# b1 rows loaded in W1's queue and transposed alone, 21 matmuls into the first layer

## The chip, the cores and the metric

The kernel runs on one core of a Trainium2 chip. The metric is device microseconds of one execution. Every execution also has a span, from the first to the last instruction of its profile; all times "at" below are microseconds from the span's start. The metric is about 2 us longer than the span.

## The reference, cut to what matters

The input x has 2048 rows of 640. A gate mixes two branches: a diagonal complex state-space layer (A) and a two-layer network (B).

```python
h = jnp.einsum("bsd,df->bsf", x, w1) + b1          # B: 640 -> 1728, bias b1
h = _gelu(h)
b = jnp.einsum("bsf,fd->bsd", h, w2) + b2          # back to 640
Lam_bar = jnp.exp(dt * Lam)                        # A: 640 states, dt = exp(log_dt)
# ... Bu = x B_bar^T; h_t = Lam_bar h_(t-1) + Bu_t; a = 2 Re(h C^T) + x Dskip
return g * a + (1 - g) * b                         # g = sigmoid(sum(x * gate_w))
```

Two kinds of small vectors are needed as columns, one value per partition: Lambda_re, Lambda_im and log_dt (15 rows of 128) for the tables of branch A, and b1 (13.5 rows of 128, padded to 14) as the bias of the GELU after the first layer.

## The kernel before: the parts that matter

Every operation is put to a list scheduler, which works with estimated durations (`dur`, `lat`) and priorities (`prio`) when the kernel is built, and fixes the program order of each engine. A late estimate therefore gives a late place in program order, whatever happens on the chip.

The small rows are loaded from ACT's queue; one TensorE transpose turns all 29 rows into columns, and VectorE copies them out of PSUM:

```python
for i, (nm, src) in enumerate((("lre", A_Lambda_re), ("lim", A_Lambda_im), ("ldt", A_log_dt))):
    load(nm, "act", ..., rows[i * KP:(i + 1) * KP, :], src..., [("rows", i)], prio=-100 + i, dur=0.45)
load("b1a", "act", ..., rows[3 * KP:NR - 1, :], B_b1[0:nmain]..., ["b1a"], prio=-97, dur=0.4, lat=2.5)
for h in range(2):                                  # the last half row, twice
    load(f"b1b{h}", "act", ..., rows[NR - 1:NR, h * 64:h * 64 + FL], ..., [("b1b", h)], prio=-96 + h, dur=0.4, lat=2.5)
# ... cut
def f_cols():
    return inc("pe", nc.tensor.transpose(psC[:, 0:NR], rows[:, :], ident[0:NR, 0:NR]))
op("cols", "pe", 0.2, [("rows", 0), ("rows", 1), ("rows", 2), "b1a", ("b1b", 0), ("b1b", 1), "ident"], [("bank", 7)], f_cols, prio=-855)
def f_cols1():
    return inc("dve", nc.vector.tensor_copy(out=cols[:, :], in_=psC[:, 0:NR]))
op("cols1", "dve", 0.2, [("bank", 7)], ["lcol", "b1col"], f_cols1, prio=-3000)
```

x's first 512 rows come in two halves (SP's queue), are transposed by 20 TensorE transposes and copied by VectorE to xT. Then the first layer starts, 35 matmuls of 128x512, block k of W1 after block k:

```python
def m1_first():
    for k in range(KD):                             # KD = 5
        for jf in ((5, 6, 0, 1, 2, 3, 4) if k == 0 else range(NW)):   # NW = 7
            # matmul(PS[jf], W1sb[:, k, jf*128:(jf+1)*128], xT[:, k, 0:512]), prio 1, 2, ... 35
    # ... cut: GELU of the 7 banks with b1col as bias
```

SP's queue issues, in this order: x (2), W1's blocks (5), W1's rest, B (10 DMA transposes), xT block 1 (5), W2, xT blocks 2 and 3 (5), C (10).

## Time and profile before

| | |
|---|---|
| time, median of 3 (range) | 217.86 us (217.44 to 218.26) |
| span of the profiled execution | 215.8 us |
| TensorE matmul (PE) busy | 212.0 us, 98% |
| VectorE (DVE) busy | 191.4 us, 89% |
| chain of waits | PE 96%, DMA 2% |

The page of the kernel before, the busy time of the engines (share of the span, number of instructions) and the shares of the chain that ended last:

```profile
...
PE 212.0 (98%) x1286; PEld 124.2 (58%) x1286; DVE 191.4 (89%) x268; ACT 99.3 (46%) x169; POOL 4.6 (2%) x13
...
PE 96%; DMA 2%; SPq 0%; DVE 0%; issue 0%
...
```

PE is busy for 98% of the span and makes 96% of the chain. Nothing is to be had from any other engine unless PE waits for it.

The timeline of the head (start, duration, engine, line, operation, out<-in, count; in brackets the idle time ahead of it and its releaser):

```profile
...
3.73 2.34 PE L413 MATMUL ps<-ident,xn 128*128 128x128 bf16 x20
...
5.25 1.09 DVE L420 COPY xT<-ps 128x512 bf16<-128x512 bf16 x3 [2.25 <-PE ps L413]
...
6.57 0.59 PE L611 MATMUL ps<-xT,W1sb 128*128 128x512 bf16 x2 [0.51 <-DMA W1sb<-in_B_w_dram]
...
7.09 0.18 PE L430 MATMUL ps<-ident,rows 29*128 29x29 bf16 x1
...
7.21 7.30 PE L611 MATMUL ps<-xT,W1sb 128*128 128x512 bf16 x33
7.32 0.19 DVE L435 CAST cols<-ps 128x29 f32<-128x29 bf16 x1 [0.98 <-PE ps L430]
...
11.34 0.32 DVE L479 TENSOR_TENSOR tr<-tr 128x165 f32<-128x165 f32 x1
...
14.34 6.64 PE L630 MATMUL ps<-xT,W1sb 128*128 128x512 bf16 x30
...
```

L413 are the x transposes, L611 the first layer, L430 the transpose of the 29 rows. It stands after the second matmul of the layer. The first matmul waits 0.51 us for a DMA of W1, not for xT, whose first copy ran from 5.25. The tables of branch A start with the copy of the columns at 7.32 (L435); their long coefficient block starts at 11.34.

The chain of waits over the head (start, duration, what):

```profile
...
1.76 4.67 DMA W1sb<-in_B_w_dram
6.43 0.14 issue
6.57 0.59 PE ps L611 x2
7.16 0.12 PE ps L430
7.28 7.23 PE ps L611 x33
14.51 6.47 PE ps L630 x30
...
```

The start of the first layer is the landing of W1's first block, issued at 1.76 and landed at 6.43. From there on the chain is PE alone.

### The profile page before, as it was taken

Reading aid. Unit: us, or ns where it says so; the run is one execution under the profiler, and the core shown is the slowest. Engines: PE = TensorE matmul, PEld = TensorE weight load, DVE = VectorE, ACT = ScalarE, POOL = GpSimd, SP = SyncE. Lnnn points to the kernel's source line nnn. Section 1 sums busy time; section 2 is a strip of 40 time slices with the busy share of each in tenths; the row PEclk is TensorE's granted clock in tenths of the full one; section 3 lists DMA queues with packets and bytes.
Section 4 is the critical chain, followed back from the end, with each engine's and each line's share of the span. In section 5 each row is a group of like instructions: output and inputs, shape, how many; then the busy total and the mean of one; then the engine's idle time right before and its main releaser. Section 6 shows DMA issues by size and latency. Waiting matters only on the chain.

```text
span 215.8 us, 3288 instructions
## 1 busy us (share of the span) xinstructions
PE 212.0 (98%) x1286; PEld 124.2 (58%) x1286; DVE 191.4 (89%) x268; ACT 99.3 (46%) x169; POOL 4.6 (2%) x13
## 2 busy tenths in 40 slices
PE   8999999999999999999999999999999999999995
PEld 4444444444577776444457777544447777777774
DVE  3799999999999999999996999799999999996313
ACT  2478556665533224556653322556662233233220
POOL 1010030000000100000000010000000000000000
DMA  6987579995610140000000013000000000001001
GB/s 191 350 158 138 93 204 338 235 126 122 124 31 30 34 149 2 30 0 0 3 0 0 33 37 147 30 3 0 0 0 3 1 34 28 30 30 33 30 30 30
DMA packets 28201, 15.44 MB, mean 72 GB/s; under 512 B 22044, under 2 KB 27740, under 8 KB 28188
## 3 DMA queue, kind: packets, MB, share of 16 engines
q1 hardware_dynamic: 27568, 12.95, 24.7%
q0 software_dynamic: 560, 2.30, 3.4%
q8 instruction: 10, 0.16, 0.3%
q14 instruction: 3, 0.02, 0.0%
q10 hardware_dynamic: 60, 0.01, 0.0%
HBM read 7.38 MB, written 2.62 MB: 46 GB/s over the span
## 4 chain that ended last, share of the span: by engine, by line
PE 96%; DMA 2%; SPq 0%; DVE 0%; issue 0%
PE ps L750 26%; PE ps L630 23%; PE ps L776 20%; PE ps L675 20%; PE ps L611 4%; DMA W1sb<-in_B_w_dram 2%; PE ps L751 2%; PE ps L651 1%; SPq L330 0%; DVE osb L809 0%; PE ps L430 0%
## 5 line engine op out<-in xcount | busy, mean ns | idle before, releaser
L750 PE MATMUL ps<-W2sb,Gl 128*128 128x320 bf16 x416 | 61.4, 299 | 0.0
L750 PEld LDWEIGHTS ps<-W2sb,Gl 128*128 128x128 bf16 x416 | 40.5, 98 | 16.6 <-issue 0.4
L630 PE MATMUL ps<-xT,W1sb 128*128 128x512 bf16 x225 | 49.2, 379 | 0.0
L776 PE MATMUL ps<-CT,H 128*128 128x320 bf16 (+2 forms) x330 | 46.1, 295 | 0.0
L715 DVE TENSOR_TENSOR_SCAN W<-atab,V 128x1280 bf16<-128x1280 f32 x16 | 44.3, 2811 | 0.3
L675 PE MATMUL ps<-xT,BT 128*128 128x512 bf16 x200 | 43.8, 379 | 0.0
L776 PEld LDWEIGHTS ps<-CT,H 128*128 128x128 bf16 x330 | 31.7, 98 | 12.0
L638 ACT ACTIVATE Gl<-ps,cols 128x512 bf16<-128x512 f32 x45 | 30.6, 692 | 16.1 <-PE ps L630 16.1
L630 PEld LDWEIGHTS ps<-xT,W1sb 128*128 128x128 bf16 x225 | 22.0, 98 | 26.6
L675 PEld LDWEIGHTS ps<-xT,BT 128*128 128x128 bf16 x200 | 19.5, 98 | 23.5 <-issue 0.4
L684 ACT ACTIVATE U<-ps 128x512 bf16<-128x512 f32 x40 | 23.9, 597 | 18.3 <-PE ps L675 18.3
L795 DVE SCALAR_TENSOR_TENSOR xg<-xn,gcol,dsk 128x640 bf16<-128x640 bf16 x16 | 13.9, 883 | 0.4
L758 ACT ACTIVATE E_0<-ps,g1col 128x320 bf16<-128x320 f32 x12 | 6.3, 527 | 16.5 <-PE ps L751 16.5
L590 DVE SCALAR_TENSOR_TENSOR scr<-xn,gwb 128x640 bf16<-128x640 bf16 x16 | 13.2, 822 | 0.4
L479 DVE TENSOR_TENSOR H<-H,V 128x1280 bf16<-128x1280 bf16 x16 | 12.5, 822 | 0.3
L479 DVE TENSOR_TENSOR V<-V,W 128x1280 bf16<-128x1280 bf16 x16 | 12.5, 821 | 0.3
L479 DVE TENSOR_TENSOR V<-mr,U 128x2560 bf16<-128x2560 bf16 x8 | 11.9, 1490 | 0.5 <-DVE s L479 0.2
L479 DVE TENSOR_TENSOR H<-c,W 128x2560 bf16<-128x2560 bf16 x8 | 11.9, 1489 | 0.1
L479 DVE TENSOR_TENSOR V<-s,W 128x2560 bf16<-128x2560 bf16 x8 | 11.9, 1484 | 0.0
L479 DVE TENSOR_TENSOR W<-mi,U 128x2560 bf16<-128x2560 bf16 x8 | 11.9, 1484 | 0.0
L758 ACT ACTIVATE E_2<-ps,g1col 128x320 bf16<-128x320 f32 x10 | 5.3, 527 | 13.6 <-PE ps L751 13.6
L758 ACT ACTIVATE E_1<-ps,g1col 128x320 bf16<-128x320 f32 x10 | 5.3, 528 | 12.9 <-PE ps L751 12.9
(89 smaller groups left out, 124.6 us busy)
## 6 DMA issues: line engine op xcount, KB each, us to landing
out_dram<-osb SPq DMA_DIRECT2D x15, 160.0 KB, 1.8
W2sb<-in_B_w_dram SPq DMA_DIRECT2D x1, 2080.0 KB, 12.7
xn<-in_A_x_dram POOLq DMA_DIRECT2D x3, 640.0 KB, 4.8
W1sb<-in_B_w_dram SPq DMA_DIRECT2D x5, 224.0 KB, 4.8
W1sb<-in_B_w_dram SPq DMA_DIRECT2D x1, 1040.0 KB, 7.5
xn<-in_A_x_dram SPq DMA_DIRECT2D x2, 320.0 KB, 3.0
xT<-in_A_x_dram SPq DMA_TRANSPOSE x10, 4.6
dsk<-in_A_Dskip_dram POOLq DMA_DIRECT2D x1, 160.0 KB, 6.9
```

The costliest lines, as they stand in the source:

```text
L479: return inc("dve", nc.vector.tensor_tensor(out=o, in0=a, in1=b, op=o_))
L590: t = inc("dve", nc.vector.scalar_tensor_tensor(out=scr[:, :], in0=xn[q % 2][:, c, :], scalar=1.0, in1=gwb[:, :], op0=ALU.mult, op1=ALU.mu ...
L611: return inc("pe", nc.tensor.matmul(PS[jf][:, :], W1sb[:, k, jf * 128:(jf + 1) * 128], xT[:, k, 0:512], start=(k == 0), stop=(k == KD - 1)))
L630: t = nc.tensor.matmul(PS[bank][:, :], W1sb[:, k, jf * 128:(jf + 1) * 128], xT[:, k, q * 512:(q + 1) * 512], start=(k == 0), stop=(k == KD ...
L638: return inc("act", nc.scalar.activation(Gl[q % 2][:, jf, :], PS[bank][:, :], ACT.Gelu_apprx_tanh, bias=b1col[:, jf:jf + 1]))
L675: t = nc.tensor.matmul(PS[bank][:, :], BT[:, kd, ci, k * 128:(k + 1) * 128], xT[:, kd, q * 512:(q + 1) * 512], start=(kd == 0), stop=(kd = ...
L684: return inc("act", nc.scalar.activation(dst, src, ACT.Copy, scale=1.0 if ci == 0 else -1.0))
L715: t = inc("dve", nc.vector.tensor_tensor_scan(out=g[:, ci, :], data0=a, data1=v[:, ci, :], initial=0.0, op0=ALU.mult, op1=ALU.add))
L750: t = nc.tensor.matmul(PS[bank][:, 0:HALF], Gl[q % 2][:, jf, ts], W2sb[:, jf, cols], start=(jf == 0), stop=False)
L758: return inc("act", nc.scalar.activation(E1[c % NE][:, cols], PS[bank][:, 0:HALF], ACT.Copy, scale=g1col[:, c:c + 1]))
L776: t = nc.tensor.matmul(PS[bank][:, 0:n], H[b % NHB][:, ci, k, s * 128:(s + 1) * 128], CT[:, k, ci, cols], start=(i == 0), stop=(i == 2 * K ...
L795: return inc("dve", nc.vector.scalar_tensor_tensor(out=xg[c % 2][:, :], in0=xn[q % 2][:, c % 4, :], scalar=gcol[:, c:c + 1], in1=dsk[:, :] ...
```

## The change

Intent: the transpose of Lambda and dt no longer waits for b1, so it can run before the first layer and the tables of branch A can start earlier; b1, which is not needed before the first GELU at 13, is loaded later, out of ACT's queue, and transposed by itself 21 matmuls into the layer.

```diff
-        rows = SB("rows", [NR, 128], BF16)
-        cols = SB("cols", [128, NR], FP32)
+        rows = SB("rows", [3 * KP, 128], BF16)
+        b1rows = SB("b1rows", [NF, 128], BF16)
+        cols = SB("cols", [128, 3 * KP], FP32)
+        b1col = SB("b1col", [128, NF], FP32)
 ...
-        load("b1a", "act", ..., prio=-97, dur=0.4, lat=2.5)
-        for h in range(2):
-            load(f"b1b{h}", "act", ..., prio=-96 + h, dur=0.4, lat=2.5)
+        load("b1a", "sp", "l_b1a", b1rows[0:NF - 1, :], B_b1[0:nmain]..., ["b1a"], prio=6.2, dur=0.3, lat=2.5)
+        load("b1b", "sp", "l_b1b", b1rows[NF - 1:NF, :]..., B_b1[nmain:F]....broadcast_to([1, 2, FL]), ["b1b"], prio=6.3, dur=0.3, lat=2.5)
 ...
-            return inc("pe", nc.tensor.transpose(psC[:, 0:NR], rows[:, :], ident[0:NR, 0:NR]))
-        op("cols", "pe", 0.2, [("rows", 0), ("rows", 1), ("rows", 2), "b1a", ("b1b", 0), ("b1b", 1), "ident"], ...)
+            return inc("pe", nc.tensor.transpose(psC[:, 0:3 * KP], rows[:, :], ident[0:3 * KP, 0:3 * KP]))
+        op("cols", "pe", 0.2, [("rows", 0), ("rows", 1), ("rows", 2), "ident"], ...)
 ...
+        def f_colb():
+            return inc("pe", nc.tensor.transpose(psC[:, 0:NF], b1rows[:, :], ident[0:NF, 0:NF]))
+        op("colb", "pe", 0.1, ["b1a", "b1b", "ident"], [("bank", 7)], f_colb, prio=21.5)
+        def f_colb1():
+            return inc("dve", nc.vector.tensor_copy(out=b1col[:, :], in_=psC[:, 0:NF]))
+        op("colb1", "dve", 0.2, [("bank", 7)], ["b1col"], f_colb1, prio=-1000)
```

More of the change, by code (lines that the diff above doesn't have):

```diff
@@ L240, in bass_gated_mix__ssm_conv_s5__dense_activation_gelu__prompt_kernel @@
         gwb = SB("gwb", [128, D], BF16)
-        NR = 3 * KP + NF
-        rows = SB("rows", [NR, 128], BF16)
-        cols = SB("cols", [128, NR], FP32)
-        lcol = cols[:, 0:3 * KP].rearrange("p (a k) -> p a k", a=3)
-        b1col = cols[:, 3 * KP:NR]
+        rows = SB("rows", [3 * KP, 128], BF16)
+        b1rows = SB("b1rows", [NF, 128], BF16)
+        cols = SB("cols", [128, 3 * KP], FP32)
+        lcol = cols[:, :].rearrange("p (a k) -> p a k", a=3)
+        b1col = SB("b1col", [128, NF], FP32)
         dtb = SB("dtb", [128, KP], BF16)
@@ L358, in bass_gated_mix__ssm_conv_s5__dense_activation_gelu__prompt_kernel @@
             load(nm, "act", "l_" + nm, rows[i * KP:(i + 1) * KP, :], src.rearrange("(k p) -> k p", p=128), [("rows", i)], prio=-100 + i, dur=0.45)
-        load("b1a", "act", "l_b1a", rows[3 * KP:NR - 1, :], B_b1[0:nmain].rearrange("(j p) -> j p", p=128), ["b1a"], prio=-97, dur=0.4, lat=2.5)
-        for h in range(2):
-            load(f"b1b{h}", "act", f"l_b1b{h}", rows[NR - 1:NR, h * 64:h * 64 + FL], B_b1[nmain:F].rearrange("(j p) -> j p", j=1), [("b1b", h)],
-                 prio=-96 + h, dur=0.4, lat=2.5)
+        load("b1a", "sp", "l_b1a", b1rows[0:NF - 1, :], B_b1[0:nmain].rearrange("(j p) -> j p", p=128), ["b1a"], prio=6.2, dur=0.3, lat=2.5)
+        load("b1b", "sp", "l_b1b", b1rows[NF - 1:NF, :].rearrange("j (h p) -> j h p", h=2),
+             B_b1[nmain:F].rearrange("(j h p) -> j h p", j=1, h=1).broadcast_to([1, 2, FL]), ["b1b"], prio=6.3, dur=0.3, lat=2.5)
         def f_iota():
@@ L429, in f_cols @@
         def f_cols():
-            return inc("pe", nc.tensor.transpose(psC[:, 0:NR], rows[:, :], ident[0:NR, 0:NR]))
-        op("cols", "pe", 0.2, [("rows", 0), ("rows", 1), ("rows", 2), "b1a", ("b1b", 0), ("b1b", 1), "ident"], [("bank", 7)], f_cols, prio=-855)
+            return inc("pe", nc.tensor.transpose(psC[:, 0:3 * KP], rows[:, :], ident[0:3 * KP, 0:3 * KP]))
+        op("cols", "pe", 0.2, [("rows", 0), ("rows", 1), ("rows", 2), "ident"], [("bank", 7)], f_cols, prio=-855)
         def f_cols1():
-            return inc("dve", nc.vector.tensor_copy(out=cols[:, :], in_=psC[:, 0:NR]))
-        op("cols1", "dve", 0.2, [("bank", 7)], ["lcol", "b1col"], f_cols1, prio=-3000)
+            return inc("dve", nc.vector.tensor_copy(out=cols[:, :], in_=psC[:, 0:3 * KP]))
+        op("cols1", "dve", 0.2, [("bank", 7)], ["lcol"], f_cols1, prio=-3000)
+        def f_colb():
[4 more added lines that the diff above has]
+        op("colb1", "dve", 0.2, [("bank", 7)], ["b1col"], f_colb1, prio=-1000)
         def f_dt():
```

## The prediction

> **What bounds the kernel.** TensorE. The page has PE busy 212.0 of 215.8 us (98%), and the chain of waits is PE for 96%, DMA 2%. VectorE is 89% busy, but the table of waits shows no PE wait on it after the first layer has begun. Time can be won only in the first 6.6 us, or where something is squeezed between matmuls.
>
> The head, from the timeline, the chain and the trace's records of DMA semaphores: the x halves land at 3.57 and 4.51 us; 20 transposes run 3.73 to 6.07; the first matmul starts at 6.57, released by the first W1 block, which lands at 6.44 (the chain shows 4.67 us of that DMA). xT block 0 is copied by about 5.7, so that side has 0.7 us of slack. The transpose of the 29 rows stands after the second matmul: matmuls start 0.216 us apart, the third would start at 7.00 and starts at 7.21. So it costs PE about 0.2 us (0.12 on the chain). All its rows had landed by 5.81 (b1) and 4.49 (Lambda, dt): no wait, just a late place in program order. The Trainium skill, "TensorE: Matmul & The Clock Gate", Step-by-step, says matmuls stay in program order, only weight loads are pulled ahead; this fits.
>
> **What the change does.**
> 1. Three b1 loads leave ACT's queue (0.92 us of issue, nothing waits for it).
> 2. Two small loads enter SP's queue behind W1's five blocks: about 0.3 us of issue each, so W1's rest and the B transposes are issued 0.6 us later. W1's rest landed at 11.71, first used 14.34: slack 2.6. B_re is used from 20.82, landed 16.64; B_im used about 26.4, landed 23.79; xT1 used 31.6, landed 29.20. All have 2 us or more. The b1 rows stand in ring order behind W1 (the skill, "DMA: Bandwidth & Descriptors", Queues, rings and completion order), whose fifth block landed at 8.71: I estimate 9 us, before their transpose at about 11.2.
> 3. The Lambda/dt transpose no longer waits for b1; the list scheduler should place it between the two halves of the x transposes. Rows landed at 4.49, its turn is about 4.8: no stall. It delays the second half by 0.15 to 0.3 us, inside the 0.7 us of slack.
> 4. A new 14-row transpose sits after 21 matmuls: about 0.1 to 0.2 us of PE, the same as is removed.
> 5. VectorE: the first COPY to cols moves from 7.32 to about 5.2; the Lambda chain (dtb, acol, angles) starts about 0.8 us earlier. But the new b1 copy is queued ahead of the long coefficient block and waits for the transpose (about 11.4), so VectorE idles about 0.8 us there and the block starts at about 11.6, against 11.34. The gain is given back. The tables then end within 0.4 us of 33.7, and their first user is far from PE's path (first H ready at 49, needed 61.5).
>
> **Sum.** Out of the first layer about -0.2 us, into it +0.15; start unchanged (6.57, W1). Net 0 to -0.1 us; the spread of the three runs (217.44 to 218.26) is larger. Predicted 217.8 us, range 217.2 to 218.4; faster by over 2% 1%, within 2% 98%, slower 1%.
>
> **To check.** First matmul 6.4 to 6.7; Lambda transpose before 5.2; one gap of about 0.1 to 0.2 us after matmul 21; VectorE idle just before the b1 copy with TensorE's transpose as releaser; last first-layer matmul ends at 14.5; PE share 98%.
>
> **What would make it wrong.** The small rows in ACT's queue landing late, holding the x transposes past 6.4 (PE start moves one for one); b1 landing after 11 behind the 128-partition W1 blocks, stalling PE; the b1 copy placed behind the coefficient block, holding banks for 2 us; a different order later.

## The result

The changed kernel takes 217.51 us (median of 6, 217.20 to 217.69); the kernel before takes 217.82 us (6 runs, 217.44 to 218.26). The ratio is 0.9986, 95% interval 0.9972 to 1.0000. A ratio is the mean time of one kernel's runs over that of the other's of the same rounds, so it is not quite the ratio of the medians quoted.

The page of the changed kernel, the same lines (its lines of code have moved: first layer L621, x transposes L412, Lambda transpose L429, b1 transpose L439):

```profile
...
PE 212.0 (98%) x1287; PEld 123.6 (57%) x1287; DVE 191.5 (89%) x269; ACT 99.3 (46%) x169; POOL 4.6 (2%) x13
...
PE 96%; DMA 2%; SPq 0%; DVE 0%; issue 0%
...
```

The timeline of its head:

```profile
...
3.96 1.24 PE L412 MATMUL ps<-ident,xn 128*128 128x128 bf16 x10
...
5.12 0.18 PE L429 MATMUL ps<-ident,rows 15*128 15x15 bf16 x1
...
5.23 0.73 PE L412 MATMUL ps<-ident,xn 128*128 128x128 bf16 x10
5.34 0.17 DVE L434 CAST cols<-ps 128x15 f32<-128x15 bf16 x1 [2.34 <-PE ps L429]
...
6.57 4.71 PE L621 MATMUL ps<-xT,W1sb 128*128 128x512 bf16 x21 [0.60 <-DMA W1sb<-in_B_w_dram]
...
11.21 0.18 PE L439 MATMUL ps<-ident,b1rows 14*128 14x14 bf16 x1
...
11.42 0.17 DVE L444 CAST b1col<-ps 128x14 f32<-128x14 bf16 x1 [0.86 <-PE ps L439]
11.51 0.56 DVE L489 TENSOR_TENSOR tr<-tr 128x165 f32<-128x165 f32 x2
...
14.35 6.64 PE L640 MATMUL ps<-xT,W1sb 128*128 128x512 bf16 x30
...
```

The chain of waits over its head:

```profile
...
1.76 4.67 DMA W1sb<-in_B_w_dram
6.43 0.14 issue
6.57 4.71 PE ps L621 x21
11.28 0.11 PE ps L439
11.39 3.13 PE ps L621 x14
14.51 6.47 PE ps L640 x30
...
```

The two chains agree to the hundredth: W1's first block lands at 6.43 in both, the layer starts at 6.57 in both, and the next layer starts on the chain at 14.51 in both. One small transpose has gone from matmul 2 to matmul 21 (0.12 and 0.11 us on the chain). On VectorE the first column copy moved from 7.32 to 5.34 and the table chain ran ahead, but the b1 copy (L444) stands in front of the coefficient block and waited 0.86 us for the b1 transpose; the block started at 11.51 in place of 11.34. So the profiles show the whole change, and none of the 0.3 us: the spans are 215.8 before and 215.9 after. What was left to find out was whether the 0.3 us are real, and if so where they lie.

### The profile page after: what moved, and what is told of

Its sections match the earlier page's. It is cut to its first block, busy times and chain, and to the rows that moved or that the text cites. A ratio compares the mean times of both kernels' runs of the same rounds, so it can differ in the third digit from the quotient of the medians.

```text
span 215.9 us, 3291 instructions
## 1 busy us (share of the span) xinstructions
PE 212.0 (98%) x1287; PEld 123.6 (57%) x1287; DVE 191.5 (89%) x269; ACT 99.3 (46%) x169; POOL 4.6 (2%) x13
## 4 chain that ended last, share of the span: by engine, by line
PE 96%; DMA 2%; SPq 0%; DVE 0%; issue 0%
PE ps L760 26%; PE ps L640 22%; PE ps L786 20%; PE ps L685 20%; PE ps L621 4%; DMA W1sb<-in_B_w_dram 2%; PE ps L761 2%; PE ps L661 1%; SPq L330 0%; DVE osb L819 0%; PE ps L439 0%
## 5 line engine op out<-in xcount | busy, mean ns | idle before, releaser
L786 PE MATMUL ps<-CT,H 128*128 128x320 bf16 (+2 forms) x330 | 46.1, 295 | 0.0
L786 PEld LDWEIGHTS ps<-CT,H 128*128 128x128 bf16 x330 | 31.7, 98 | 12.1 <-DMA CT<-in_A_C_im_dram 0.2
L648 ACT ACTIVATE Gl<-ps,b1col 128x512 bf16<-128x512 f32 x45 | 30.6, 692 | 16.1 <-PE ps L640 16.1
L768 ACT ACTIVATE E<-ps,g1col 128x320 bf16<-128x320 f32 x32 | 16.9, 528 | 43.0 <-PE ps L761 43.0
L797 ACT ACTIVATE E<-ps,gcol 128x320 bf16<-128x320 f32 x30 | 15.8, 527 | 25.0 <-PE ps L786 25.0
L489 DVE TENSOR_TENSOR osb<-xg,E 128x640 bf16<-128x640 bf16 x15 | 7.3, 487 | 10.1 <-ACT E L797 10.0
```

The costliest lines, as they stand in the source:

```text
L489: return inc("dve", nc.vector.tensor_tensor(out=o, in0=a, in1=b, op=o_))
L648: return inc("act", nc.scalar.activation(Gl[q % 2][:, jf, :], PS[bank][:, :], ACT.Gelu_apprx_tanh, bias=b1col[:, jf:jf + 1]))
L768: return inc("act", nc.scalar.activation(E1[c % NE][:, cols], PS[bank][:, 0:HALF], ACT.Copy, scale=g1col[:, c:c + 1]))
L786: t = nc.tensor.matmul(PS[bank][:, 0:n], H[b % NHB][:, ci, k, s * 128:(s + 1) * 128], CT[:, k, ci, cols], start=(i == 0), stop=(i == 2 * K ...
L797: return inc("act", nc.scalar.activation(E2[c % NE][:, cols], PS[bank][:, 0:HALF], ACT.Copy, scale=gcol[:, c:c + 1]))
```

## The experiments

**Theory T1**: TensorE bounds the kernel, its start is gated by W1, and the change puts into the first layer what it takes out; no gain inside the span. **Rival R1**: something real is freed inside the span that two profiles did not happen to show. Later: **T2**, on the time outside the span.

One execution of each kernel was profiled. This table gathers from those traces what decides a span: when W1's first block (in c3 and d1 its first piece) had landed, from the trace's record of DMA semaphores; the start of the first W1 matmul; the time from there to the start of the next layer; the landing of the C transposes; and the time from the first W1 matmul to the first second-layer matmul behind the first C group. From the first C matmul to the end of the last matmul all fourteen traces have the same 151.78 to 151.80 us, and 2.48 to 2.50 from there to the span's end, so a span is decided by these columns. (The zero of this table lies up to 0.02 us before that of the views, so 6.43 there can be 6.44 here.)

| trace | W1 block landed | first W1 matmul | first layer | C landed | start to behind C | span |
|---|---|---|---|---|---|---|
| before | 6.44 | 6.57 | 7.77 | 60.62 | 57.70 | 215.8 |
| b1, before again | 6.54 | 6.67 | 7.77 | 60.82 | 57.69 | 215.9 |
| changed | 6.44 | 6.58 | 7.78 | 61.56 | 57.76 | 215.9 |
| a1, changed again | 5.51 | 5.92 | 7.80 | 61.21 | 58.06 | 215.5 |
| a2 | 5.98 | 6.33 | 7.81 | 60.05 | 57.74 | 215.6 |
| a3 | 6.24 | 6.37 | 8.44 | 60.87 | 58.36 | 216.3 |
| a4 | 5.94 | 6.08 | 8.04 | 60.86 | 57.96 | 215.6 |
| b2 | 5.76 | 6.25 | 7.79 | 51.06 | 57.71 | 215.5 |
| b3 | 6.31 | 6.44 | 7.78 | 60.65 | 57.71 | 215.7 |
| b4 | 6.22 | 6.36 | 7.55 | 61.34 | 57.75 | 215.6 |
| c1 | 5.66 | 5.99 | 7.80 | 58.77 | 57.72 | 215.3 |
| c2 | 5.83 | 6.33 | 7.56 | 51.47 | 57.49 | 215.4 |
| c3 | 5.24 | 5.91 | 7.56 | 52.70 | 57.49 | 214.9 |
| d1 | 5.93 | 6.07 | 7.55 | 53.10 | 57.48 | 215.1 |

And this one the times. "Outside" is the mean of time minus span over a kernel's runs. Kernels of one letter shared a chip and the runs of the kernel before.

| kernel | ratio to before, 95% | median us | before, median us | median span | before's span | outside, us | before's outside |
|---|---|---|---|---|---|---|---|
| changed | 0.9986 (0.9972 to 1.0000) | 217.51 | 217.82 | 215.7 | | 1.79 | |
| a1 | 0.9975 (0.9945 to 1.0004) | 217.24 | 217.54 | 215.45 | 215.5 | 1.79 | 1.98 |
| a2 | 0.9982 (0.9949 to 1.0015) | 217.40 | 217.54 | 215.4 | 215.5 | 1.97 | 1.98 |
| a3 | 1.0015 (0.9985 to 1.0046) | 218.08 | 217.54 | 215.9 | 215.5 | 2.13 | 1.98 |
| a4 | 0.9989 (0.9959 to 1.0020) | 217.46 | 217.54 | 215.65 | 215.5 | 1.80 | 1.98 |
| b1 | 0.9992 (0.9974 to 1.0009) | 217.45 | 217.61 | 215.45 | 215.6 | 1.94 | 1.99 |
| b2 | 0.9983 (0.9967 to 0.9999) | 217.20 | 217.61 | 215.4 | 215.6 | 1.80 | 1.99 |
| b3 | 0.9987 (0.9970 to 1.0004) | 217.34 | 217.61 | 215.55 | 215.6 | 1.79 | 1.99 |
| b4 | 1.0004 (0.9986 to 1.0023) | 217.68 | 217.61 | 215.6 | 215.6 | 2.04 | 1.99 |
| c1 | 1.0006 (0.9981 to 1.0031) | 217.76 | 217.62 | 215.8 | 215.6 | 1.96 | 2.01 |
| c2 | 0.9980 (0.9958 to 1.0002) | 217.24 | 217.62 | 215.3 | 215.6 | 1.95 | 2.01 |
| c3 | 0.9967 (0.9945 to 0.9990) | 216.91 | 217.62 | 214.95 | 215.6 | 1.94 | 2.01 |
| d1 | 0.9989 (0.9971 to 1.0006) | 217.46 | 217.50 | 215.5 | 215.6 | 1.94 | 1.95 |

In the a runs one execution of the kernel before took 219.72 us, in the c runs one took 218.90 us; they widen those intervals and lower those ratios, and medians are the better guide there. For the first row only one execution of the kernel before has its span on record: 217.73 us with a span of 215.8, so 1.93 outside.

### a1: the changed kernel again

Edit: none.

> The changed kernel itself, a second time. Theory T1 (TensorE bounds it, its start is gated by the first W1 block, and the change takes about as much out of the first layer as it puts in): ratio to before 0.9990 to 1.0010, the 0.3 us of the first look is mostly noise. Rival R1 (the move frees something real in most executions that the two profiles do not show, for instance b1 rows that land late and hold the transpose): ratio again 0.998 to 0.9995, below 1 clear of noise.

Measured: 217.24 against 217.54, again 0.3 us less. The ratio of 0.9975 is below what either theory gave, because of the one execution of 219.72 us; the medians' ratio, 0.9986, is R1's number, but the interval holds 1. The span's medians, 215.45 and 215.5, differ by 0.05 us only. The gain is in the part outside: 1.79 us, against 1.98 in the kernel before. This was not foreseen by either theory.

The trace shows two more things. W1 landed 0.93 us earlier than in the first trace, and the layer started 0.65 us earlier. Then C held TensorE back; the chain of waits of a1 around the first C group (L786):

```profile
...
56.83 1.27 SPq L337
...
58.14 3.06 DMA CT<-in_A_C_im_dram
...
61.24 2.89 PE ps L786 x20
...
```

The chain leaves PE for the last C transpose, which landed at 61.20. From the start to behind C it took 58.06 us in place of the kernel before's 57.70: 0.36 us of an earlier start were lost to that wait.

### a2: the split alone, b1 stays in ACT's queue

```diff
-load("b1a", "sp", ..., prio=6.2, dur=0.3)
+load("b1a", "act", ..., prio=-97, dur=0.4)
-load("b1b", "sp", ..., prio=6.3, dur=0.3)
+load("b1b", "act", ..., prio=-96, dur=0.4)
```

> Two transposes as in the change, but the b1 loads stay in ACT's queue. T1: same time as the changed kernel within 0.2 us; the SP queue is 1.2 us earlier, the C transposes land about 60.6 (61.56 in the changed kernel), so the 0.05 us that TensorE lost at 61.7 is gone. R1 in the form that the gain lies in ACT's queue: as slow as before, about 0.3 us slower than the changed kernel. If the gain lies in the split: as fast as the changed kernel.

Measured: 217.40, between the two; within 0.2 us of the changed kernel, as T1 said. Span 215.4, as a1 and the kernel before; outside 1.97, as the kernel before. C landed at 60.05 and no wait was left there. The split by itself is worth nothing that can be seen.

### a3: the loads moved, one transpose

```diff
-load("b1a", "act", ..., prio=-97, ...)          # and b1b0, b1b1
+load("b1a", "sp", ..., prio=6.2, dur=0.3)       # and b1b, as in the change
# one transpose of 29 rows as before; the scheduler puts it after 9 matmuls
```

> The b1 loads move to the SP queue as in the change, but one transpose takes all 29 rows; it stands after 9 matmuls of the first layer and its last row should land near 9.1 us, when TensorE would be there at about 8.5. T1: TensorE stalls 0.6 to 0.8 us there, and the whole time grows by 0.5 to 0.8 us against before; VectorE's tables end about 2 us later (near 36) at no further cost. A rival that has VectorE's table chain on the path expects about 2 us.

The chain of waits of a3 over its head (L429 is the transpose, L610 the first layer):

```profile
...
4.16 4.64 DMA rows<-in_B_b_dram
8.80 0.28 issue
9.08 0.17 PE ps L429
9.25 5.72 PE ps L610 x26
...
```

The chain now runs through the landing of b1 at 8.80, and PE starts the transpose at 9.08 after 0.6 us of idle. The layer took 8.44 us in place of 7.77, 0.67 more, as T1 expected; the median time grew by 0.54 and the median span by 0.4. VectorE's column copy came at 9.28, 2 us later than before, and start to behind C grew by 0.66 us, no more than the layer did: VectorE's tables are not on the path. This is why the change needs its second transpose: with b1 in SP's queue, Lambda's rows must not wait for it, and b1 must be placed behind its landing.

### a4: the b1 transpose eleven times

```diff
 def f_colb():
+    for _ in range(10):
+        nc.tensor.transpose(psC[:, 0:NF], b1rows[:, :], ident[0:NF, 0:NF])
     return inc("pe", nc.tensor.transpose(psC[:, 0:NF], b1rows[:, :], ident[0:NF, 0:NF]))
```

> The changed kernel with the b1 transpose done eleven times in place of once: ten more of them measure what one costs inside the first layer. T1: about 0.07 to 0.11 us each (the chain shows 0.11 for one), so +0.7 to +1.1 us against the changed kernel, and the first layer ends later by the same. If small transposes hide under the 512-column matmuls: within 0.2 us.

The chain of waits of a4 (L440 the ten, L441 the one that was there):

```profile
...
10.78 0.33 PE ps L440 x10
11.11 0.03 PE ps L441
...
```

T1's figure is wrong, and the time bears it out: 217.46 against a1's 217.24, where 0.7 us or more were expected. Ten more transposes cost 0.25 us of the layer (8.04 against 7.78, before rounding 0.251), 25 ns each, and from the second on they start 25 ns apart; the Trainium skill, "TensorE: Matmul & The Clock Gate", Part 1, Wait — 56ns, not 53.3ns?, gives about 25 ns as the floor of the spacing of small matmuls, and this trace agrees. Yet one transpose costs far more than that: in the trace of the changed kernel the transpose starts 0.312 us after the matmul ahead of it, the next matmul 0.109 us after the transpose, the one after that 0.226 us later. Without it, two matmuls would have followed at 0.216 each: 0.647 less 0.432 is 0.215 us for a single transpose of 14 rows. The kernel before shows 0.308, 0.117 and 0.227 around its transpose of 29 rows, 0.220 us. So the price is paid once for each interruption of the stream of 512-column matmuls, not once for each transpose, and the chain's 0.11 and 0.12 show about half of it. Which part of an interruption costs it (the wait for the rows' semaphores, the small weight load or the change of shape) no run tells apart.

### b1: the kernel before again

Edit: none.

> The kernel before against itself: what noise looks like, and a second trace of it. Two traces of the changed kernel differ by 0.65 us in the start of the first W1 matmul (6.58 and 5.92) while the first W1 block landed at 6.44 and 5.51. T1: the start in this trace lies in the same range 5.9 to 6.6 and everything from the first C matmul to the end takes 151.78 us again; the time between start and first C matmul is 54.98, as C landed early. Ratio 0.999 to 1.001, and time minus span near 2.0 us (1.79 in the changed kernel): two thirds of the 0.3 us lie outside the span. Rival R1 (inside): time minus span is the same as in the changed kernel, spans differ by 0.3.

Measured: ratio 0.9992, a difference of 0.17 us in the medians between equal kernels; that is the noise against which the rest is to be read. The start in this trace is 6.67, 0.07 outside the range that T1 gave. Start to first C matmul is 54.98 again. Outside the span the six runs have 1.94 us in the mean. Against R1 stand a1's medians of the span on one chip, 215.45 and 215.5: they do not differ by 0.3. A difference of 0.15 us or less would not be seen, since here two equal kernels have 215.45 and 215.6.

### b2: C ahead of the last x block

```diff
-["CT"], prio=10, dur=14.0)
+["CT"], prio=7.9, dur=14.0)
```

> The changed kernel with the C transposes issued before the last xT block's, so they land before 56. If TensorE is held at the first C matmul by C's landing (0.05 us in the first trace of the changed kernel, 0.35 in the second): start to first C matmul is 55.0 in the trace whatever the start, and the time is 0.05 to 0.35 us below the changed kernel, 217.0 to 217.2 on this chip. If C is not on the path: the same time as the changed kernel.

C landed at 51.06 and start to behind C is 57.71, the kernel before's value, 0.05 and 0.35 us below the two traces of the changed kernel. Median 217.20 on a chip where the changed kernel itself was not run; the mean span, 215.42, cannot be told from a1's 215.40. What the traces show is the wait gone; that it pays on average is not shown.

### b3: two more small loads in SP's queue

```diff
+for i in range(2):                                # behind b1b; never used, waited for by W2's load
+    load(f"b1x{i}", "sp", ..., b1spare[i][0:NF - 1, :], B_b1[0:nmain]..., prio=6.4 + 0.01 * i)
```

> The changed kernel with two more small b1 loads (never used) behind the b1 loads in the SP queue: the cost in issue time of the move doubled, about 1.2 us more of the SP queue, a few KB more bytes. If the move has eaten the slack of the C transposes: C lands 62.0 to 62.8, TensorE stalls 0.6 to 1.5 us at the first C matmul (or earlier at B_im or xT block 1, whose slack was 0.6 to 1), and the time grows by 0.6 to 1.3 us. If the SP queue has slack of 2 us as the prediction said: within 0.2 us of the changed kernel.

I had come to believe that the change eats the slack of C: B's transposes are issued 1.2 us later and in the first trace C landed 0.94 us later. Here is SP's queue in the changed kernel:

```profile
...
4.16 1.18 SPq L330 DMA_DIRECT2D b1rows<-in_B_b_dram  x2
...
5.85 9.78 SPq L337 DMA_TRANSPOSE BT<-in_A_B_re_dram  x5
15.68 6.67 SPq L337 DMA_TRANSPOSE BT<-in_A_B_im_dram  x5
...
```

And in b3, with twice as many small loads:

```profile
...
4.16 1.20 SPq L331 DMA_DIRECT2D b1rows<-in_B_b_dram  x2
5.40 0.83 SPq L331 DMA_DIRECT2D b1spare<-in_B_b_dram  x2
...
6.71 7.23 SPq L338 DMA_TRANSPOSE BT<-in_A_B_re_dram  x5
13.99 6.52 SPq L338 DMA_TRANSPOSE BT<-in_A_B_im_dram  x5
...
```

The issue of B's transposes began 0.86 us later than in the changed kernel, and that of the first five ended 1.7 us earlier (13.94 against 15.63). Over the fourteen traces these five take 7.2 to 10.1 us to issue, and that swing swallows a microsecond; what sets it, no run shows. C landed at 60.65, the time is 217.34, and there is no stall. The theory falls; and b4 below has C at 61.34 with no b1 load in SP's queue. Over all traces with C in its old place, C lands at 60.7 in the mean both of the six with b1 in SP's queue (58.77 to 61.56) and of the four without (60.05 to 61.34). The late C of the first traces is scatter from execution to execution, not the work of the change.

### b4: one transpose, before the first matmul

```diff
 # the kernel before; only the scheduler's estimate of the landing, so only the order, changes
-load("b1a", "act", ..., lat=2.5)                  # and b1b0, b1b1
+load("b1a", "act", ..., lat=1.9)
```

> The kernel before with only the order changed: the one transpose of 29 rows stands after the x transposes and before the first W1 matmul; loads stay in ACT's queue. T1: b1 lands at 5.8, so it fits into the wait for W1 or costs up to 0.2 us before it; out of the first layer come 0.12 us (the chain's figure) : 0 to 0.2 us faster than before, ratio 0.999 to 1.000. Start to first C matmul 54.86. R1 (late b1 rows are what cost time in before): slower than before, as the first matmul then waits for b1 directly.

The timeline of PE in b4 (L413 x transposes, L430 the 29 rows, L611 the first layer):

```profile
...
3.73 1.77 PE L413 MATMUL ps<-ident,xn 128*128 128x128 bf16 x20
5.79 0.17 PE L430 MATMUL ps<-ident,rows 29*128 29x29 bf16 x1 [0.29 <-DMA rows<-in_B_b_dram]
6.35 1.89 PE L611 MATMUL ps<-xT,W1sb 128*128 128x512 bf16 x8 [0.39 <-DMA W1sb<-in_B_w_dram]
```

The transpose waited 0.29 us for b1 and was still done before W1 landed at 6.22. The layer took 7.55 us, 0.22 less than with a transpose in it, which confirms the price worked out under a4. But in this trace C landed late, start to behind C was 57.75 where 57.48 would be due (c2 to d1), and 0.27 us were given back. The median span is 215.6, as that of before; outside 2.04. No gain in time is shown.

### c1: two unused loads back in ACT's queue

```diff
+for i in range(2):                                # never used, waited for by W2's load
+    load(f"b1x{i}", "act", ..., b1spare[i][0:NF - 1, :], B_b1[0:nmain]..., prio=-97 + i, dur=0.4)
```

T2 came from the last columns of the second table: 1.79 to 1.80 us outside the span in the changed kernel, a1, a4, b2 and b3; 1.94 to 2.04 in the kernel before, a2 and b4, which have five or six loads in ACT's queue. The traces' packet records of before, a2 and b4 hold one 8192-byte packet of an instruction queue after the span's end, at 217.4 to 217.7, the others none (their last packet of any kind ends before the span does, so how far their records reach is not known). Nor does b1's trace, though it is the kernel before, and that very execution has 1.8 us outside (217.70 less 215.9).

> The changed kernel with two small loads, never used, added to ACT's queue, so that ACT's program is about as long as in the kernel before and all else stays. So far the time outside the span is 1.79 to 1.80 us in every kernel with three loads in ACT's queue and b1 split off (five of them), 1.94 to 2.04 in every one with five or six loads there (four runs), and 2.13 in the one run with the loads in SP's queue and one transpose. Theory T2 (ACT's longer program costs an instruction fetch after the last instruction, which the traces of before, of a2 and of b4 show near 217.5): time minus span goes to 1.95 to 2.05, the span stays within 0.15 us of the changed kernel's, a fetch after the span's end returns. If it stays at 1.80, the outside part has another cause.

Measured: 1.96 us outside, and the packet is there, at 217.1. The whole time is 217.76 against 217.62: ratio 1.0006, no gain is left to see, with b1 placed as in the change, though the interval still holds the change's 0.9986. Its median span, 215.8, lies 0.1 and 0.35 above the changed kernel's 215.7 and 215.45 on other chips, more than I allowed in the second case, so a part of the lost gain may be inside. So for this pair T2's number holds: two more loads in ACT's queue bring the longer part outside back. But it is no full account, as c2 shows.

### c2: b1 from POOL's queue, one transpose before the layer, C first

```diff
 # the kernel before, with
-load("b1a", "act", ..., prio=-97, ...)            # and b1b0, b1b1
+load("b1a", "pool", ..., prio=-59, dur=0.6, lat=2.3)
+load("b1b", "pool", ..., prio=-58, dur=0.6, lat=2.3)
-["CT"], prio=10, dur=14.0)
+["CT"], prio=7.9, dur=14.0)
```

> The kernel before, with the b1 rows loaded from POOL's queue, one transpose of all 29 rows after the x transposes and before the first W1 matmul, and the C transposes issued before the last xT block's. No transpose stands inside the first layer: from first W1 matmul to the next layer 7.55 us (7.77 to 7.78 in before and in the changed kernel), no stall at C: start to second-layer group after C 57.48 us in place of 57.70 to 58.06. If b1 lands by 5.5, span 215.1 to 215.3 in the mean, 0.2 to 0.4 below before. Time 217.0 to 217.3 (ratio 0.998), depending on the time outside the span: by T2 1.80, as ACT has three loads.

POOL has little to do (4.6 us busy on the page of the kernel before). The Trainium skill, "DMA: Bandwidth & Descriptors", Issuing engines are not separate DMA queues, says that another issuing engine saves sequencer time alone; here that is the point, as b1 is not to delay W1's issue or lengthen ACT's program. The trace agrees as far as it goes: SP issued W1's rest at 4.16, as in the kernel before, and not at 5.39 as in the changed kernel. The timeline of PE in c2:

```profile
3.96 2.31 PE L412 MATMUL ps<-ident,xn 128*128 128x128 bf16 x20
6.21 0.18 PE L429 MATMUL ps<-ident,rows 29*128 29x29 bf16 x1
6.32 1.90 PE L610 MATMUL ps<-xT,W1sb 128*128 128x512 bf16 x8
```

b1's rows landed at 5.01 and 5.86, the second later than the 5.5 I had asked for, but not too late: the x transposes (L412), at about 107 ns apart throughout, still ran, and they, not W1 (landed 5.83) and not b1, held the start of the layer at 6.33. The layer took 7.56 and start to behind C 57.49, both as expected. The median span is 215.3, 0.3 below before's, the time 217.24 against 217.62. But outside it has 1.95, with three loads in ACT's queue and no packet after the end: T2 predicted 1.80. a3, also with three loads there, has 2.13. So the number of loads in ACT's queue does not set the part outside. Another count, made afterwards in the traces, orders all the kernels: ACT's instructions, those of its sequencer included. a3 has 183 of them (2.13 us outside); c2, and c3 and d1 below, 184 (1.94 to 1.95); the changed kernel, a1, a4, b2 and b3 185 (1.79 to 1.80); the kernel before, a2, b4 and c1 187 (1.94 to 2.04). This is a pattern, not a test: no run was made for it, fewer is not shorter, and why it should matter the traces do not show.

### c3: W1's first block in two pieces

```diff
+load("w1_0a", "sp", ..., W1sb[:, 0, FA:FW], ...)  # columns of jf 5 and 6, which are used first; FA = 640
+load("w1_0b", "sp", ..., W1sb[:, 0, 0:FA], ...)
-load("w1_0", "sp", ..., W1sb[:, 0, 0:FW], ...)
```

> c2 with the first W1 block loaded in two pieces, the two column groups that are used first ahead of the rest. Where W1's landing gates the start (six of ten traces so far, first matmul 0.12 to 0.14 us after it), the first piece should land about 0.3 us earlier and the start is then held by the x transposes and the xT copy: first W1 matmul 5.7 to 6.2, at most a small wait after two matmuls. Span 0.1 to 0.3 us below c2. If the rest of the block then holds the third matmul as late as before, the same as c2.

The timeline of PE in c3 (L415 x transposes, L432 the 29 rows, L613 the first layer):

```profile
...
3.84 1.98 PE L415 MATMUL ps<-ident,xn 128*128 128x128 bf16 x20
5.76 0.18 PE L432 MATMUL ps<-ident,rows 29*128 29x29 bf16 x1
5.90 2.33 PE L613 MATMUL ps<-xT,W1sb 128*128 128x512 bf16 x10
```

The first piece landed at 5.24, the rest at 5.69, and PE runs from the x transposes through the small transpose into the first layer with no wait for W1. Median 216.91 against 217.62, ratio 0.9967 (0.9945 to 0.9990), span 214.95 against 215.6. Of the thirteen intervals this one and b2's, which ends at 0.9999, leave 1 out. It was not run beside the changed kernel. Nor does a trace show that the split of W1 moved the start: the second piece too had landed at 5.69, before the layer began at 5.91 (held by the first xT copy, which ended at 5.85), and c2's later start was due to its slow x transposes, not to W1.

### d1: c3 with two transposes

```diff
 # the changed kernel, with b1 from POOL's queue, C first, W1 in pieces as in c3, and
-op("colb", "pe", 0.1, ..., prio=21.5)
+op("colb", "pe", 0.1, ..., prio=-850)             # before the first W1 matmul
```

> c3 with two transposes in place of one, both before the first W1 matmul: Lambda between the halves of x, b1 (from POOL's queue) after them. Inside the span the same as c3 within noise: layer 7.55 to 7.56, start to second-layer group after C 57.49, mean span 215.0 to 215.3, time 0.3 to 0.8 us below before (ratio 0.997 to 0.9985). Outside the span it asks what c2, c3 and a3 (1.95, 1.94, 2.13 with one transpose and three loads in ACT's queue) left open: 1.80 if a separate b1 transpose and copy brings it, as in the changed kernel; 1.95 if the place of the loads does.

Layer 7.55 and 57.48, as expected. The first piece landed at 5.93 this time, and the layer started at 6.07, so the split of W1 did not keep its promise in this trace. Median 217.46 against 217.50, ratio 0.9989: the gain is below what I expected, slightly in ratio and clearly in microseconds (0.04 by the medians, 0.27 by the means). The mean span, 215.36, misses the expected 215.0 to 215.3 and is 0.3 us above c3's 215.07, with the same work in the layer. The runs of c3 and d1 scatter over 1.0 and 0.6 us of span, so how much of c3's gain repeats is open. Outside it has 1.94: a separate b1 transpose and copy do not bring the 1.80 back.

## Why the prediction was right

It said 217.8 us, 217.2 to 218.4, and 98% for within 2%; measured were 217.51 us and a ratio of 0.9986. The range is about the spread of the first three runs, so that the time fell into it says little; what tests the reasoning is the mechanism, point by point:

- **What bounds the kernel.** Right. Both chains are PE for 96%, and the start of the layer is W1's landing at 6.43 in both. In other traces that landing moves from 5.51 to 6.54, and the start with it in eight of the fourteen (0.13 to 0.14 us behind it); when it is early, the x transposes (a2, b2, c2, where all of them ran at the slow pace) or the first xT copy (a1, c1, c3) hold the start instead. So "gated by W1" held in the two first traces partly by luck.
- **0.2 us out of the layer, 0.15 into it.** Right in balance: layer 7.77 before, 7.78 after. The true price is 0.22 us at either place (b4, c2: 7.55 and 7.56 without one), so the 0.15 for the new place was set a little low.
- **Lambda's transpose between the halves, no stall.** Right: it ran at 5.12, and the first matmul stayed at 6.57.
- **VectorE's lead is given back at the b1 copy.** Right: idle 0.86 us (said: 0.8), block at 11.51 (said: 11.6). a3 shows that even 2 us there cost nothing.
- **b1 at 9 us.** Right: 8.94 and 9.12. In a1 they landed at 8.42 and 8.15, ahead of W1's fifth block (8.50), so behind W1 in the queue did not mean landing after it.
- **Two loads of about 0.3 us of issue, 0.6 us later.** Mis-sized: they took 1.18 us, and W1's rest was issued 1.2 us later. It did not matter, as b3 shows.
- **"All have 2 us or more" of slack.** Wrong as a list: it left out C, which comes last in the queue and had 0.9 us (landed 60.62, first used 61.55). In two traces, a1 and b4, C held PE for about 0.3 us, in the changed kernel's first for 0.05. In that trace B_im and xT block 1 also landed 1.6 and 1.8 us later than before, where 0.6 was said, but not in a1. The runs put this down to scatter, not to the change.
- **Net 0 to -0.1 us.** Inside the span that holds: 215.45 against 215.5 in a1. The time fell by 0.3 us in both jobs, and in a1 the rest, 0.2 us, lies outside the span, which the prediction never looked at. c1 takes this part away again with two unused loads in ACT's queue. Why is not settled: an instruction packet after the span's end goes with it in the traces of kernels with five or six loads in ACT's queue (run b1 has neither), but a3, c2, c3 and d1 have the long end without the packet; the count of ACT's instructions orders them all, untested. A rival inside the span is not excluded either: W1 landed at 6.0 in the mean of the six traces with b1 in SP's queue and ACT's queue left short, at 6.3 in the four with b1 in ACT's queue, with a scatter from 5.5 to 6.5; but c1, with two loads back in ACT's queue, has 5.66.

## What to carry to other kernels

On an engine that is busy 98% of the time, moving a small operation from one place in its stream to another gained nothing here; taking it out of the stream shortened the layer by more than its own length, by 0.22 us for a transpose that adds 0.025 us once others are beside it. Put such things where the engine waits anyway, here ahead of the first W1 matmul, and look what the earlier end then runs into (b4 gave the gain back at C). And before a difference of 0.1% is explained from a profile, split each time into span and remainder: in a1, two thirds of it were never in the profile.

## What the Trainium skill lacked or had wrong

- "TensorE: Matmul & The Clock Gate", Part 2, Back-to-back issue gap, gives about 131 ns per 512-column matmul as the sustained rate with weight loads. Every trace here has a median of 216 ns in its W1 layers, weight loads and all, the value that the page calls the isolated gap and that its Part 1 measures.
- The same page, Part 4, says that the full clock does not engage for transposes. Here the x transposes start 106 to 107 ns apart in some stretches and 55 to 56 ns in others. In eight traces the step comes among them (the changed kernel and runs a1, b1, b3, b4, c1, c3, d1), in a4 right after the first, and in five (the kernel before's first, a2, a3, b2, c2) all 20 ran at the slow pace. That it comes at a different moment in each run agrees with Part 1, What's actually happening (a free-running window). Seven warm-up matmuls of 128x512 run ahead of the transposes in all of them, so whether transposes alone would bring the fast pace is not shown.
- No page gives the price of one small transpose inside a stream of 512-column matmuls: 0.22 us for the first, 0.025 for each further one.
- "Runtime: NRT & Kernel Launch", The ~15µs preamble/postamble breakdown, speaks of a kernel-invariant gap of about 6.2 us between a profile's total and the reported time. The quantities here are others (device time and span, and here the profile's is the shorter), but their gap is 1.79 to 2.13 us and does depend on the program, by more than the change is worth inside the span; no page says on what (for the count that it goes with here, see c2).
